# Weights loaded back to back in 8 KB runs, and the second product moved ahead: a schedule change in a fused retention and gated MLP kernel

## The chip, the cores and the metric

The kernel runs on one core of a Trainium2 chip. The metric is device time in microseconds (us), lower is better. All times are of single executions; a kernel's figure is the median of its executions, and each experiment ran in rounds beside the kernel before on the same chip. A run is called slow when it lies more than 1.5% above the fastest run of its kernel; verdicts use the fast runs alone.

## The reference, cut to what matters

```python
# q, k, v: (4 batches, 8 heads, 768 steps, 64)
for t in range(S):                                    # retention, a decay gamma per head
    state = gamma * state + outer(k[:, :, t], v[:, :, t])
    y[:, :, t] = scale * q[:, :, t] @ state
x = y as (3072 tokens, 512)
h = x @ w_in                                          # 512 x 2048
out = (h * cos(h)) @ w_out                            # 2048 x 512
```

The kernel works in *pairs*: pair p is one chunk of 128 steps for two batches, 12 pairs in all. Two pairs make a *group* of 512 tokens, 6 groups. For a pair TensorE does T (transposes of q and k), A (scores), after a mask on VectorE Y (output), and the state. For a group it then does F (x times w_in, 16 units of four 512-column matmuls, each followed by a cosine on ScalarE and a product on VectorE) and O (times w_out, 16 units of four matmuls). F and O units are nearly all of TensorE's work.

## The kernel before: the parts that matter

```python
w_in_sb = sb([128, KIN, DF], BF16, "w_in_sb")      # KIN = 4, DF = 2048
w_out_sb = sb([128, KOUT, DM], BF16, "w_out_sb")   # KOUT = 16, DM = 512

def load_w_in(r, n=512):                           # piece r: 512 columns
    nc.gpsimd.dma_start(
        out=w_in_sb[:, :, ts(r, n)],
        in_=moe_w_in[:, ts(r, n)].rearrange("(i p) f -> p i f", p=128))

def load_w_out(r):
    nc.gpsimd.dma_start(
        out=w_out_sb[:, ts(r, 4), :],
        in_=moe_w_out[ts(r, 512), :].rearrange("(f p) m -> p f m", p=128))
# ... cut ...
def unit_f(g, f):                                  # one F unit of a group
    bank = banks.take()
    for i in range(KIN):
        nc.tensor.matmul(bank, lhsT=w_in_sb[:, i, ts(f, 128)], rhs=xt[g % 2][:, i, :],
                         start=(i == 0), stop=(i == KIN - 1))
    act(bank, gt[g % 2][:, f, :])
    banks.give(bank)
# pair_f(p, r): the same for one pair, four units of 256 columns for piece r
# ... cut ...
load(nc.gpsimd, 1, ("k0", "q1", "k1", "v1"))       # DMA order: w_in between the pairs
load_w_in(0, 256)
load_w_in(1, 256)
load_w_in(1)
# ... loads of pairs 2 to 4, load_w_in(2), load_w_in(3), and only then:
for r in range(4):
    load_w_out(r)
# ... TensorE's order: pair 0, pair 1, F of group 0, pair 2, part of F, pair 3, F of group 1,
#     then O of group 0 beside pairs 4 and 5, then F of g and O of g-1 in turns
```

Of the kernel before, what the change touches and what calls it, by code (L numbers as in the profile page):

```python
# [30 lines left out]
def kernel(  # L31
# [9 lines left out]
    nc = tc.nc  # L41
# [8 lines left out]
    NP = B // 2 * NC  # L50
    NG = NP // 2
    PRE = 5
    PT = 5

    scale = 1.0 / math.sqrt(D)
    lg = [math.log(1.0 - 2.0 ** (-5.0 - h)) for h in range(H)]
# [10 lines left out]
    banks = Banks([psum.tile([128, 512], FP32, name=f"bank{i}") for i in range(7)])  # L67
# [37 lines left out]
    def load(eng, p, names):  # L105
        bp, c = divmod(p, NC)
        for n in names:
            t, src = SRC[n[0]]
            b = int(n[1])
            eng.dma_start(  # L110
                out=t[p % PRE][b],
                in_=src[2 * bp + b, :, ds(c * C, C)].rearrange("h t d -> t h d"))

    def load_w_in(r, n=512):
# [4 lines that stand above are left out]
    def load_w_out(r):  # L119
        nc.gpsimd.dma_start(  # L120
            out=w_out_sb[:, ts(r, 4), :],
            in_=moe_w_out[ts(r, 512), :].rearrange("(f p) m -> p f m", p=128))


    nc.gpsimd.iota(pos, pattern=[[C, NC]], base=1, channel_multiplier=1,
                   allow_small_or_imprecise_dtypes=True)
    load(nc.sync, 0, ("q0", "k0", "q1"))
    load(nc.sync, 1, ("q0", "v0"))
    load(nc.gpsimd, 0, ("k1", "v0", "v1"))
    make_identity(nc, ident)  # L130
    nc.vector.memset(zero, 0.0)
    nc.vector.memset(lnsc, math.log(scale))
# [17 lines left out]
    def conv_q(p, eng):  # L150
        for b in range(2):
            eng.tensor_tensor(out=qs[p % NB][:, b], in0=qf[p % PRE][b],  # L152
                              in1=bc(gq, p % NC), op=ALU.mult)

    def conv_v(p, eng):
        for b in range(2):
            eng.tensor_tensor(out=vs[p % NB][:, b], in0=vf[p % PRE][b],  # L157
                              in1=bc(gk, p % NC), op=ALU.mult)

    def conv_k(p, on_act):  # L160
        for b in range(2):
            if on_act:
                nc.scalar.copy(out=ks[p % NB][:, b], in_=kf[p % PRE][b])  # L163
            else:
                nc.vector.tensor_copy(out=ks[p % NB][:, b], in_=kf[p % PRE][b])

    def stage_t(p, split, fill=0):
        n = p % NB
        for b in range(2):
            if fill:  # L170
                warm(fill * b)
            bank = banks.take()
            tr = bank.bitcast(BF16).rearrange("p (w a t) -> p w a t", w=2, a=HP)
            for w, src in enumerate((qs[n], ks[n])):
                for a in range(HP):
                    nc.tensor.transpose(tr[:, w, a, :], src[:, b, 2 * a : 2 * a + 2, :], ident)
            if split is None or split and b == 1:
                nc.vector.tensor_copy(out=qkt[n][:, :, b], in_=tr)  # L178
            else:
                nc.scalar.copy(out=qkt[n][:, :, b], in_=tr)  # L180
            banks.give(bank)

    def stage_t_dma(p):
        n = p % NB
        for w, src in enumerate((qs[n], ks[n])):
            nc.sync.dma_start_transpose(
                out=qkt[n][:, w].rearrange("p b a t -> p (b a) t"),
                in_=src.rearrange("p b h d -> p (b h d)"))
# [75 lines left out]
    def unit_f(g, f):  # L264
        bank = banks.take()
        for i in range(KIN):
            nc.tensor.matmul(bank, lhsT=w_in_sb[:, i, ts(f, 128)], rhs=xt[g % 2][:, i, :],  # L267
                             start=(i == 0), stop=(i == KIN - 1))
        act(bank, gt[g % 2][:, f, :])
        banks.give(bank)  # L270

    def pair_f(p, r, parts=(0, 1)):

        g, hf = divmod(p, 2)
        for f in [4 * r + 2 * i for i in parts]:
            bank = banks.take()
            for e in range(2):
                for i in range(KIN):
                    nc.tensor.matmul(bank[:, ts(e, 256)], lhsT=w_in_sb[:, i, ts(f + e, 128)],  # L279
                                     rhs=xt[g % 2][:, i, ts(hf, 256)],  # L280
                                     start=(i == 0 and e == 0), stop=(i == KIN - 1),
                                     skip_group_check=True)
            act(bank, gt[g % 2][:, f : f + 2, ts(hf, 256)])
            banks.give(bank)
# [2 lines left out]

    def unit_o(g, j, part):
        if part == 0:
            o_bank[0] = banks.take()  # L290
        bank = o_bank[0]
        for f in range(4 * part, 4 * part + 4):
            nc.tensor.matmul(bank, lhsT=gt[g % 2][:, f, ts(j, 128)], rhs=w_out_sb[:, f, :],  # L293
                             start=(f == 0), stop=(f == KOUT - 1))
        if part == 3:
            o = ob[j % 4]
            bp, c = divmod(2 * g + j // 2, NC)
            dst = out[ds((2 * bp + j % 2) * S + c * C, C), :]
            if g == NG - 1 and j == 3:
                nc.vector.tensor_copy(out=o[:, ts(0, 256)], in_=bank[:, ts(0, 256)])  # L300
                nc.sync.dma_start(out=dst[:, ts(0, 256)], in_=o[:, ts(0, 256)])
                nc.scalar.copy(out=o[:, ts(1, 256)], in_=bank[:, ts(1, 256)])
                nc.scalar.dma_start(out=dst[:, ts(1, 256)], in_=o[:, ts(1, 256)])
            else:
                nc.scalar.copy(out=o, in_=bank)  # L305
                nc.sync.dma_start(out=dst, in_=o)
            banks.give(bank)
# [10 lines left out]
    def masks(p, items):  # L318
        for it in items:
            stage_m(p, it)  # L320

    load(nc.gpsimd, 1, ("k0", "q1", "k1", "v1"))
    load_w_in(0, 256)
    load_w_in(1, 256)
    load_w_in(1)
    load(nc.sync, 2, ("q0", "q1"))
    load(nc.sync, 4, ("q0", "q1", "v0"))
    conv_v(1, nc.gpsimd)
    load_w_in(2)
    load(nc.gpsimd, 2, ("k0", "k1"))  # L330
    load_w_in(3)
    load(nc.gpsimd, 2, ("v0", "v1"))
    load(nc.gpsimd, 3, ("k0", "q0", "k1", "q1"))
    conv_q(2, nc.gpsimd)
    conv_v(2, nc.gpsimd)
    load(nc.gpsimd, 3, ("v0", "v1"))
    for r in range(4):
        load_w_out(r)

    warm(10)  # L340
    conv_q(0, nc.vector)
# [7 lines left out]
    conv_q(1, nc.vector)  # L349
    warm(6)  # L350
    stage_y(0, nc.scalar.copy)
    conv_v(3, nc.gpsimd)
    load(nc.gpsimd, 4, ("k0", "k1", "v1"))
    warm(2)
    stage_t(1, None)
    m1 = stage_a(1)
# [2 lines left out]
    banks.give(spare)  # L359
    stage_y(1, nc.scalar.copy)  # L360
    pair_f(1, 0)
    for r in (1, 2):
        pair_f(0, r)
        pair_f(1, r)
    conv_k(2, True)
    pair_f(0, 3)
    stage_t(2, None)
    pair_f(1, 3, (0,))
    m2 = stage_a(2)
    masks(2, m2)  # L370
    pair_f(1, 3, (1,))
    stage_y(2, nc.scalar.copy)
    load(nc.sync, 5, ("q0", "q1", "v0"))
    conv_q(4, nc.gpsimd)
    load(nc.gpsimd, 5, ("k0", "k1", "v1"))
    pair_f(2, 0)
    conv_k(3, True)
    conv_q(3, nc.vector)
    pair_f(2, 1)
    stage_t(3, None)  # L380
    pair_f(2, 2, (0,))
    m3 = stage_a(3)
    masks(3, m3)
    pair_f(2, 2, (1,))
    pair_f(2, 3)
    stage_y(3, nc.scalar.copy)
    conv_v(4, nc.gpsimd)
    load(nc.sync, 6, ("q0", "q1", "v0"))
    load(nc.gpsimd, 6, ("k0", "k1", "v1"))
    for r in range(4):  # L390
        pair_f(3, r)
        if r == 2:
            conv_k(4, True)


    todo = []
    for g in range(1, NG + 1):
        for s in range(16):
            hf, r = divmod(s, 8)
            p = 2 * (g + 1) + hf  # L400
            if 1 < g < NG:
                unit_f(g, s)
            unit_o(g - 1, *divmod(s, 4))
            if p < NP:
                if r == 0 and p + 1 < NP:
                    conv_q(p + 1, nc.gpsimd)
                    conv_k(p + 1, True)
                    conv_v(p + 1, nc.gpsimd)
                elif r == 1 and p < PT:
                    stage_t(p, False)  # L410
                elif r == 2:
                    todo = stage_a(p)
                    stage_m(p, todo[0])
                    if PT <= p + 1 < NP:
                        stage_t_dma(p + 1)
                elif r == 3:
                    stage_m(p, todo[1])
                elif r == 6:
                    stage_y(p)
                    if p + 3 < NP:  # L420
                        load(nc.sync, p + 3, ("q0", "q1", "v0"))
                        load(nc.gpsimd, p + 3, ("k0", "k1", "v1"))


# [28 lines left out]
```

## Time and profile before

| | before |
|---|---|
| time, median of 3 (lowest to highest) | 219.75 us (219.67 to 219.83) |
| span of the profiled run, TensorE busy | 217.8 us, 94% |
| first F matmul | 15.8 us |
| first O matmul | 59.0 us |
| TensorE without a named wait from | about 63.7 us to the end |

These are three rows of the profile page's part 2 (the span in 40 slices of 5.4 us; a digit is the busy share in tenths; PEclk is the clock granted to TensorE, 9 meaning full or nearly; DMA is the load of the transfer engines):

```profile
PE   7687987879999999999999999999999999999993
...
PEclk9999999999999999999999999999999999999999
DMA  6999999999969999996951651051011001110212
```

TensorE is full from the tenth slice on; what is missing lies in the first 50 us, where the DMA engines are full too. The timeline of TensorE shows the waits (start, length, what, count, and in brackets the idle time ahead of it and what ended it). In these views PE is TensorE, PEld its weight loads, DVE VectorE, ACT ScalarE, POOL GpSimd and SPq Sync's queue. Of the tiles, qf, kf and vf are the loaded q, k and v, qs, ks and vs their converted forms, qkt the transposes, am the masked scores, xt the output Y as F reads it, gt the product h cos(h), and bank a buffer for matmul results:

```profile
15.80 1.05 PE L279 MATMUL bank<-xt,w_in_sb 128*128 128x256 bf16 x8
17.81 1.05 PE L279 MATMUL bank<-xt,w_in_sb 128*128 128x256 bf16 x8 [0.97 <-DMA w_in_sb<-in_moe_w_in_dram]
...
30.41 1.92 PE L279 MATMUL bank<-xt,w_in_sb 128*128 128x256 bf16 x16 [0.91 <-DMA w_in_sb<-in_moe_w_in_dram]
...
44.75 0.40 PE L176 MATMUL bank<-ident,qs 128*128 128x128 bf16 x4 [0.83 <-DVE qs L152]
...
58.99 1.89 PE L293 MATMUL bank<-w_out_sb,gt 128*128 128x512 bf16 x8
```

Each piece of w_in is waited for about 1 us at a time, and between 33 and 48 us it is conversions and copies on other engines that TensorE waits for. O, which needs little from the others, starts only at 59 us. The weight loads (LDWEIGHTS) and the 256-column matmuls that read w_in (duration in ns as min/median/max):

```profile
L279 PEld LDWEIGHTS <-w_in_sb x256: 95/98/99, 15.8 to 58.8; 128*128 128x128 bf16 x128
L279 PE MATMUL bank<-xt,w_in_sb x256: 269/273/283, 15.8 to 58.9; 128*128 128x256 bf16 x128
```

### The profile page before, as it was taken

To read this page: it belongs to the slowest core of one execution; us is meant where nothing else is said; L and a number is where in the kernel's file an instruction comes from. 1 tells how busy PE (TensorE), PEld (TensorE's weight loads), DVE (VectorE), ACT (ScalarE), POOL (GpSimd) and SP (SyncE) were. 2 spreads that over 40 slices of the span, in tenths; PEclk is the share of its full clock that TensorE was granted. 3 is DMA by queue.
4 is the path that set the end of the run, shared out by engine and by line. 5 is a ranking of instruction groups with operands and counts; after the bars stand their busy time and mean duration, and the time that the engine had idled before them with its cause. 6 is when DMAs were issued, how large, how long until landed. Compare 5 with 4: busy or idle time off the path is not lost.

```text
span 217.8 us, 4276 instructions
## 1 busy us (share of the span) xinstructions
PE 203.8 (94%) x1701; PEld 111.8 (51%) x1701; DVE 114.1 (52%) x185; ACT 116.1 (53%) x185; POOL 85.8 (39%) x98
## 2 busy tenths in 40 slices
PE   7687987879999999999999999999999999999993
PEld 2356875758855454544544544544544544444441
DVE  4595769596662417557448547647546244433000
ACT  5656784838874174464474564564534644454120
POOL 7969469982499991858160510000000000000000
PEclk9999999999999999999999999999999999999999
DMA  6999999999969999996951651051011001110212
GB/s 154 336 239 196 245 306 285 177 196 255 267 188 226 277 243 277 250 305 138 282 147 62 137 144 48 3 144 50 3 48 48 14 38 48 48 51 2 96 68 76
DMA packets 58676, 33.31 MB, mean 153 GB/s; under 512 B 48224, under 2 KB 53088, under 8 KB 58656
## 3 DMA queue, kind: packets, MB, share of 16 engines
q1 hardware_dynamic: 50480, 17.96, 34.8%
q0 software_dynamic: 8032, 14.95, 27.3%
q8 instruction: 13, 0.21, 0.4%
q10 hardware_dynamic: 144, 0.13, 0.2%
q14 instruction: 7, 0.06, 0.1%
HBM read 27.26 MB, written 6.29 MB: 154 GB/s over the span
## 4 chain that ended last, share of the span: by engine, by line
PE 75%; DMA 10%; DVE 5%; ACT 4%; POOL 2%; SPq 1%; issue 1%; DVEq 0%; ACTq 0%; POOLq 0%
PE bank L293 37%; PE bank L267 26%; DMA w_in_sb<-in_moe_w_in_dram 6%; PE bank L279 5%; DMA vf<-in_v_dram 4%; PE bank L205 2%; PE bank L228 2%; PE bank L233 2%; DVE gt L262 2%; ACT cosb L258 2%; SPq L110 1%; DVE am L214 1%; POOL vs L157 1%; DVE qkt L178 1%; DVE qs L152 1%
## 5 line engine op out<-in xcount | busy, mean ns | idle before, releaser
L262 DVE TENSOR_TENSOR gt<-bank,cosb 128x512 bf16<-128x512 f32 x96 | 65.9, 690 | 70.4 <-ACT cosb L258 70.4
L258 ACT ACTIVATE cosb<-bank,halfpi 128x512 bf16<-128x512 f32 x96 | 65.8, 687 | 63.2 <-PE bank L267 49.9
L293 PE MATMUL bank<-w_out_sb,gt 128*128 128x512 bf16 x384 | 94.3, 379 | 0.0
L267 PE MATMUL bank<-xt,w_in_sb 128*128 128x512 bf16 x256 | 65.8, 379 | 0.0
L293 PEld LDWEIGHTS <-gt 128*128 128x128 bf16 x384 | 37.2, 98 | 44.3
L267 PEld LDWEIGHTS <-w_in_sb 128*128 128x128 bf16 x256 | 24.1, 98 | 28.3
L279 PE MATMUL bank<-xt,w_in_sb 128*128 128x256 bf16 x256 | 29.6, 273 | 3.2 <-DMA w_in_sb<-in_moe_w_in_dram 1.9
L214 DVE TENSOR_TENSOR am<-bank,mask 128x512 bf16<-128x512 f32 x48 | 30.2, 682 | 4.5 <-issue 2.5
L157 POOL TENSOR_TENSOR vs<-vf,gk 128x512 bf16<-128x512 f32 x22 | 22.9, 1059 | 13.5 <-PE bank L279 7.4
L279 PEld LDWEIGHTS <-w_in_sb 128*128 128x128 bf16 x256 | 24.5, 98 | 6.9 <-DMA w_in_sb<-in_moe_w_in_dram 2.4
L152 POOL TENSOR_TENSOR qs<-qf,gq 128x512 bf16<-128x512 f32 x18 | 19.1, 1081 | 21.1 <-DMA qf<-in_q_dram 15.5
L110 POOL DMA_DIRECT2D kf<-in_k_dram x23 | 20.9, 910 | 3.2 <-DMA w_in_sb<-in_moe_w_in_dram 2.9
L305 ACT COPY ob<-bank 128x512 f32<-128x512 f32 x23 | 13.5, 586 | 16.3 <-PE bank L293 16.3
L237 ACT CAST xt<-bank 128x512 bf16<-128x512 f32 x24 | 13.0, 588 | 10.2 <-PE bank L233 10.2
L163 ACT CAST ks<-kf 128x512 bf16<-128x512 f32 x24 | 13.7, 615 | 4.2 <-DMA kf<-in_k_dram 4.2
L110 POOL DMA_DIRECT2D vf<-in_v_dram x15 | 13.3, 891 | 1.0 <-DMA w_out_sb<-in_moe_w_out_dram 1.0
L233 PE MATMUL bank<-am,vs 128*64 128x128 bf16 x192 | 12.1, 220 | 0.9 <-DVE am L214 0.9
L250 DVE CAST stb<-st_ps 64x512 bf16<-64x512 f32 x12 | 8.3, 689 | 6.5 <-PE st_ps L245 6.3
L228 PEld LDWEIGHTS <-stb 128*64 128x64 bf16 x160 | 8.7, 109 | 4.4 <-issue 4.4
L233 PEld LDWEIGHTS <-vs 128*64 128x64 bf16 x192 | 10.1, 110 | 1.5 <-issue 0.9
L228 PE MATMUL bank<-qkt,stb 128*64 128x128 bf16 x160 | 10.6, 222 | 0.0
L205 PE MATMUL bank<-qkt 64*128 64x128 bf16 x192 | 8.3, 218 | 2.1 <-DVE qkt L178 1.6
(38 smaller groups left out, 72.3 us busy)
## 6 DMA issues: line engine op xcount, KB each, us to landing
kf<-in_k_dram POOLq DMA_DIRECT2D x23, 256.0 KB, 5.9
out_dram<-ob SPq DMA_DIRECT2D x23, 256.0 KB, 2.1
qf<-in_q_dram SPq DMA_DIRECT2D x21, 256.0 KB, 7.2
vf<-in_v_dram POOLq DMA_DIRECT2D x15, 256.0 KB, 5.9
vf<-in_v_dram SPq DMA_DIRECT2D x9, 256.0 KB, 7.7
w_out_sb<-in_moe_w_out_dram POOLq DMA_DIRECT2D x4, 512.0 KB, 13.5
w_in_sb<-in_moe_w_in_dram POOLq DMA_DIRECT2D x3, 512.0 KB, 11.7
qf<-in_q_dram POOLq DMA_DIRECT2D x3, 256.0 KB, 8.7
```

What stands on the lines that cost most here:

```text
L110: eng.dma_start(out=t[p % PRE][b], in_=src[2 * bp + b, :, ds(c * C, C)].rearrange("h t d -> t h d"))
L152: eng.tensor_tensor(out=qs[p % NB][:, b], in0=qf[p % PRE][b], in1=bc(gq, p % NC), op=ALU.mult)
L157: eng.tensor_tensor(out=vs[p % NB][:, b], in0=vf[p % PRE][b], in1=bc(gk, p % NC), op=ALU.mult)
L163: nc.scalar.copy(out=ks[p % NB][:, b], in_=kf[p % PRE][b])
L214: nc.vector.tensor_tensor(out=am[p % 2][b][j], in0=ap[j], in1=mask.unsqueeze(1).to_broadcast([128, HP, 128]), op=ALU.mult)
L228: nc.tensor.matmul(yp[ts(j, 64), a, :], lhsT=stb[p % 2][:, b, a, ts(j, 64)], rhs=qt(n, b, a), start=True, stop=False, skip_group_check=True)
L233: nc.tensor.matmul(yp[ts(j, 64), a, :], lhsT=vs[n][:, b, 2 * a + j, :], rhs=am[p % 2][b][j][:, a, :], start=(c == 0), stop=True, skip_grou ...
L258: nc.scalar.activation(out=cb, in_=bank, func=AF.Sin, bias=halfpi)
L262: nc.vector.tensor_tensor(out=out, in0=bank, in1=cb, op=ALU.mult)
L267: nc.tensor.matmul(bank, lhsT=w_in_sb[:, i, ts(f, 128)], rhs=xt[g % 2][:, i, :], start=(i == 0), stop=(i == KIN - 1))
L279: nc.tensor.matmul(bank[:, ts(e, 256)], lhsT=w_in_sb[:, i, ts(f + e, 128)], rhs=xt[g % 2][:, i, ts(hf, 256)], start=(i == 0 and e == 0), s ...
L293: nc.tensor.matmul(bank, lhsT=gt[g % 2][:, f, ts(j, 128)], rhs=w_out_sb[:, f, :], start=(f == 0), stop=(f == KOUT - 1))
```

## The change

Its intent: give TensorE work that needs no other engine (O of group 0) while pairs 2 and 3 arrive. For that w_out must come early, so it is loaded right behind w_in, and in runs of 8 KB: partition p now holds rows 4p to 4p+3 of each block of 512. The F units must then use the matching columns of w_in, every fourth one, so its weight loads are strided by 8 bytes. O of group 1 is split, eight units ahead of group 2's turn and eight within it, and pair 4's transpose goes from TensorE to DMA.

```diff
-    PT = 5
+    PT = 4
@@ load_w_out
-            in_=moe_w_out[ts(r, 512), :].rearrange("(f p) m -> p f m", p=128))
+            in_=moe_w_out[ts(r, 512), :].rearrange("(p j) m -> p j m", j=4))
+
+    w_in_f = w_in_sb.rearrange("p i (r m j) -> p i r j m", r=4, j=4)
+
+    def w_in_t(i, f):
+        return w_in_f[:, i, f // 4, f % 4, :]
@@ loads of pairs 0 to 2 reordered (cut) @@ unit_f, pair_f
-            nc.tensor.matmul(bank, lhsT=w_in_sb[:, i, ts(f, 128)], rhs=xt[g % 2][:, i, :],
+            nc.tensor.matmul(bank, lhsT=w_in_t(i, f), rhs=xt[g % 2][:, i, :],
@@ order of the DMA queue
-    load_w_in(0, 256)
-    load_w_in(1, 256)
-    load_w_in(1)
-    (pairs 2 to 4 and w_in pieces 2 and 3 in turns, cut)
+    for r in range(4):
+        load_w_in(r)
     conv_v(1, nc.gpsimd)
     for r in range(4):
         load_w_out(r)
+    (loads of pairs 2, 3, 4, cut)
@@ order of TensorE's work
     pair_f(0, 0)
     banks.give(spare)
     stage_y(1, nc.scalar.copy)
     pair_f(1, 0)
-    for r in (1, 2):
-        pair_f(0, r)
-        pair_f(1, r)
+    for f in range(4, 16):
+        unit_f(0, f)
+    (conversions of pair 2)
+    for part in range(4):
+        for j in range(2):
+            unit_o(0, j, part)
+    unit_o(0, 2, 0)
+    unit_o(0, 2, 1)
     stage_t(2, None)
+    (rest of O of group 0 between A and Y of pair 2; then pair 3 in F of group 1, cut)
+    attend(4)
+    o_units(1, 0, 4)
+    later(4)
+    attend(5)
+    ahead(6)              # conversions of pair 6
+    stage_t_dma(6)        # its transposes, on Sync's DMA queue
+    o_units(1, 4, 8)
+    later(5)
+    (then F of g and O of g-1 in turns as before; 8 O units in group 2's turn)
```

More of the change, by code (lines that the diff above doesn't have):

```diff
@@ L121, in load_w_out @@
             out=w_out_sb[:, ts(r, 4), :],
-            in_=moe_w_out[ts(r, 512), :].rearrange("(f p) m -> p f m", p=128))
+            in_=moe_w_out[ts(r, 512), :].rearrange("(p j) m -> p j m", j=4))
+    w_in_f = w_in_sb.rearrange("p i (r m j) -> p i r j m", r=4, j=4)
+    def w_in_t(i, f):
+        return w_in_f[:, i, f // 4, f % 4, :]
+    load(nc.sync, 0, ("q0", "k0", "q1"))
+    load(nc.sync, 1, ("q0", "v0"))
+    load(nc.sync, 2, ("q0", "q1", "v0"))
+    load(nc.gpsimd, 0, ("k1",))
     nc.gpsimd.iota(pos, pattern=[[C, NC]], base=1, channel_multiplier=1,
                    allow_small_or_imprecise_dtypes=True)
-    load(nc.sync, 0, ("q0", "k0", "q1"))
-    load(nc.sync, 1, ("q0", "v0"))
-    load(nc.gpsimd, 0, ("k1", "v0", "v1"))
+    load(nc.gpsimd, 0, ("v0", "v1"))
     make_identity(nc, ident)
@@ L278, in pair_f @@
                 for i in range(KIN):
-                    nc.tensor.matmul(bank[:, ts(e, 256)], lhsT=w_in_sb[:, i, ts(f + e, 128)],
+                    nc.tensor.matmul(bank[:, ts(e, 256)], lhsT=w_in_t(i, f + e),
                                      rhs=xt[g % 2][:, i, ts(hf, 256)],
@@ L289, in unit_o @@
         if part == 0:
-            o_bank[0] = banks.take()
-        bank = o_bank[0]
+            o_bank[j] = banks.take()
+        bank = o_bank[j]
         for f in range(4 * part, 4 * part + 4):
@@ L322 @@
     load(nc.gpsimd, 1, ("k0", "q1", "k1", "v1"))
-    load_w_in(0, 256)
-    load_w_in(1, 256)
-    load_w_in(1)
-    load(nc.sync, 2, ("q0", "q1"))
-    load(nc.sync, 4, ("q0", "q1", "v0"))
-    conv_v(1, nc.gpsimd)
-    load_w_in(2)
-    load(nc.gpsimd, 2, ("k0", "k1"))
-    load_w_in(3)
-    load(nc.gpsimd, 2, ("v0", "v1"))
-    load(nc.gpsimd, 3, ("k0", "q0", "k1", "q1"))
-    conv_q(2, nc.gpsimd)
-    conv_v(2, nc.gpsimd)
-    load(nc.gpsimd, 3, ("v0", "v1"))
+    for r in range(4):
+        load_w_in(r)
+    conv_v(1, nc.gpsimd)
     for r in range(4):
         load_w_out(r)
+    load(nc.sync, 3, ("q0", "q1"))
+    load(nc.gpsimd, 2, ("k0", "k1", "v1"))
+    load(nc.gpsimd, 3, ("k0", "k1", "v0", "v1"))
+    load(nc.sync, 4, ("q0", "q1"))
+    load(nc.gpsimd, 4, ("k0", "k1", "v0", "v1"))
     warm(10)
@@ L351 @@
     stage_y(0, nc.scalar.copy)
-    conv_v(3, nc.gpsimd)
-    load(nc.gpsimd, 4, ("k0", "k1", "v1"))
     warm(2)
@@ L361 @@
     pair_f(1, 0)
-    for r in (1, 2):
-        pair_f(0, r)
-        pair_f(1, r)
+    for f in range(4, 16):
+        unit_f(0, f)
     conv_k(2, True)
-    pair_f(0, 3)
+    conv_q(2, nc.vector)
+    conv_v(2, nc.vector)
+    for part in range(4):
[3 more added lines that the diff above has]
+    unit_o(0, 2, 1)
     stage_t(2, None)
-    pair_f(1, 3, (0,))
+    unit_o(0, 2, 2)
     m2 = stage_a(2)
     masks(2, m2)
-    pair_f(1, 3, (1,))
+    conv_k(3, True)
@@ L372 @@
+    unit_o(0, 2, 3)
+    load(nc.sync, 5, ("q0", "q1", "v0"))
+    load(nc.gpsimd, 5, ("k0", "k1", "v1"))
+    for part in range(3):
+        unit_o(0, 3, part)
     stage_y(2, nc.scalar.copy)
-    load(nc.sync, 5, ("q0", "q1", "v0"))
+    unit_o(0, 3, 3)
+    conv_q(3, nc.vector)
+    conv_v(3, nc.gpsimd)
     conv_q(4, nc.gpsimd)
-    load(nc.gpsimd, 5, ("k0", "k1", "v1"))
+    conv_v(4, nc.gpsimd)
     pair_f(2, 0)
-    conv_k(3, True)
-    conv_q(3, nc.vector)
+    stage_t(3, None)
     pair_f(2, 1)
-    stage_t(3, None)
@@ L381 @@
-    pair_f(2, 2, (0,))
     m3 = stage_a(3)
     masks(3, m3)
-    pair_f(2, 2, (1,))
+    conv_k(4, True)
+    stage_t_dma(4)
+    load(nc.sync, 6, ("q0", "q1", "v0"))
+    load(nc.gpsimd, 6, ("k0", "k1", "v1"))
+    pair_f(2, 2)
     pair_f(2, 3)
     stage_y(3, nc.scalar.copy)
-    conv_v(4, nc.gpsimd)
-    load(nc.sync, 6, ("q0", "q1", "v0"))
-    load(nc.gpsimd, 6, ("k0", "k1", "v1"))
-    for r in range(4):
-        pair_f(3, r)
-        if r == 2:
-            conv_k(4, True)
-    todo = []
@@ L397, with attend, ahead, later @@
-    for g in range(1, NG + 1):
+    conv_q(5, nc.gpsimd)
+    conv_v(5, nc.gpsimd)
+    pair_f(3, 0)
+    conv_k(5, True)
+    stage_t_dma(5)
+    for r in range(1, 4):
+        pair_f(3, r)
+    def attend(p):
+        todo = stage_a(p)
+        masks(p, todo)
+    def ahead(p):
+        if p < NP:
+            conv_q(p, nc.gpsimd)
+            conv_k(p, True)
+            conv_v(p, nc.gpsimd)
+    def later(p):
+        stage_y(p)
+        if p + 3 < NP:
+            load(nc.sync, p + 3, ("q0", "q1", "v0"))
+            load(nc.gpsimd, p + 3, ("k0", "k1", "v1"))
@@ L398, with o_units @@
+    def o_units(g, a, b):
+        for u in range(a, b):
+            unit_o(g, *divmod(u, 4))
+    attend(4)
[6 more added lines that the diff above has]
+    later(5)
+    for g in range(2, NG + 1):
         for s in range(16):
@@ L400 @@
             p = 2 * (g + 1) + hf
-            if 1 < g < NG:
+            if g < NG:
                 unit_f(g, s)
-            unit_o(g - 1, *divmod(s, 4))
+            if g > 2:
+                unit_o(g - 1, *divmod(s, 4))
+            elif s % 2:
+                unit_o(1, *divmod(8 + s // 2, 4))
             if p < NP:
-                if r == 0 and p + 1 < NP:
-                    conv_q(p + 1, nc.gpsimd)
-                    conv_k(p + 1, True)
-                    conv_v(p + 1, nc.gpsimd)
-                elif r == 1 and p < PT:
-                    stage_t(p, False)
+                if r == 0:
+                    ahead(p + 1)
                 elif r == 2:
@@ L413 @@
                     stage_m(p, todo[0])
-                    if PT <= p + 1 < NP:
+                    if p + 1 < NP:
                         stage_t_dma(p + 1)
@@ L418 @@
                 elif r == 6:
-                    stage_y(p)
-                    if p + 3 < NP:
-                        load(nc.sync, p + 3, ("q0", "q1", "v0"))
-                        load(nc.gpsimd, p + 3, ("k0", "k1", "v1"))
+                    later(p)
 _INS = ['q', 'k', 'v', 'moe_w_in', 'moe_w_out']
```

## The prediction

> **What bounds it now.** TensorE. In the chain of waits, from 63.7 us to about 214 us nearly every piece is matmuls back to back (four of 512 columns every 0.86 us), then 3.8 us of copy and store. The granted clock is 1.00. The loss is in front: between the first F matmul (15.8 us) and 63.7 us I count 38.7 us of matmul work at back-to-back rates, so 9 us of stalls, 6.5 of them after 33 us. The timeline names them: w_in landing (1.0 us at 17.8, 0.9 at 30.4), xt copies (0.4 to 0.5 each), qkt copies and masks of pair 2 (34 to 38 us), qs of pair 3 (43 to 45 us). The DMA engines are saturated until about 60 us: w_in's last piece lands at 30.4, w_out's near 55 us.
>
> **What the change does.**
> 1. DMA order: w_in in four pieces, w_out right behind, then pairs 2 to 4. In the packet records a weight piece takes 512 packets, about 3.35 us beside a full second queue; a 256 KB load issued by GpSimd 64 packets, 0.82 us. Estimate: w_in lands at 17.0, 20.4, 23.7, 27.1 us. Packets of 1 KB source take 59 ns, of 2 KB 96 ns; on that line an 8 KB run takes 320 ns, a w_out piece 2.75 us, and the last lands near 38 us (40.5 if long runs gain nothing); k1 of pair 2 at 40 us.
> 2. PE order: group 0's F finishes near 32.7 us without a wait; ten O units (8.6 us) then cover the arrival of pair 2; T2 comes at about 41.5 us. Waits of T, A, masks and Y fall between O units, which need little of ScalarE and VectorE. One transpose on PE (0.9 us) becomes a DMA transpose.
> 3. Cost: Sync's q/v loads starve. Full queues move packet for packet (153 each per us); behind 8 KB packets Sync gets fewer. q of pair 3 comes only at about 50 us; conv_q(3) then holds VectorE and T3 about 1 us.
> 4. Strided LDWEIGHTS: w_in columns are now 8 bytes apart. [...] This trace has no strided weight load. Contiguous ones keep up with a 128-column matmul per 56 ns (transposes); at double cost they hide under 216 ns (512 columns) and nearly under 109 ns (256 columns, 160 such left). At four times they would cost about 17 us.
>
> **Sum.** F(2) starts near 78 us with 136 O/F units left; the old kernel at 77 us has 145: about 7 us gained. I take off 2 us for unforeseen waits around pairs 2 and 3, and 1 us for a slower w_out.
>
> Predicted 214.8 us; 8 in 10 between 212.0 and 218.5. Faster by over 2%: 0.55, within 2%: 0.38, slower: 0.07.
>
> **What would show it.** w_out's last landing under 41 us; PE without idle from 20.6 to about 40 us; T2 at 41 to 44 us; T3 waiting on qs; span about 213 us, the last 130 us unchanged in rate; w_in's LDWEIGHTS still about 98 ns and 256-column matmuls 0.109 us apart.
>
> **What would make it wrong.** Strided weight loads slower than 110 ns; w_out slower in long runs (PE waits at O's parts); Sync starvation delaying q of pair 3 beyond 55 us; GpSimd stuck behind q of pair 4, so that DMA transposes of pairs 4 and 5 pass 67 us.

The double and fourfold costs of a weight load in point 4 are suppositions of mine, set against the spacings of 56, 109 and 216 ns in the trace of the kernel before; nothing measured stood behind the factors.

## More of the kernel before

The framework adds the semaphore waits by itself: it looks at which tile regions an instruction reads and which earlier instructions write them. (A semaphore is what such a wait names; some of the waits of the built programs are listed under "The result".)

## The result

| | before | after |
|---|---|---|
| time, median (lowest to highest) | 219.79 us (219.67 to 220.72), 4 runs | 226.89 us (226.41 to 227.17), 4 runs |
| ratio of fast runs, 95% interval | | 1.0312 (1.0277 to 1.0346) |
| span of the profiled run, mean granted clock | 217.8 us, 1.000 | 225.5 us, 0.969 |

Here and below a ratio is the mean time of one kernel's fast runs over that of the other's in the same rounds, so it is not quite the ratio of the medians quoted. I had predicted 2% faster; it became 3% slower. The rows of the profile page of the changed kernel:

```profile
PE   7760099999999999899999999999999999999992
...
PEclk9997559999999999999999999999999999999999
```

Two slices of TensorE are empty, and the clock falls to half. Behind that it is fuller than before. The timeline of TensorE in the changed kernel:

```profile
17.43 0.30 PE L286 MATMUL bank<-xt,w_in_sb 128*128 128x256 bf16 x1 [0.41 <-DMA w_in_sb<-in_moe_w_in_dram]
28.26 3.37 PE L286 MATMUL bank<-xt,w_in_sb 128*128 128x256 bf16 x15 [10.53 <-DMA w_in_sb<-in_moe_w_in_dram]
...
34.15 1.91 PE L286 MATMUL bank<-xt,w_in_sb 128*128 128x256 bf16 x16 [0.25 <-ACT xt L244]
35.89 10.52 PE L274 MATMUL bank<-xt,w_in_sb 128*128 128x512 bf16 x48
46.25 8.80 PE L300 MATMUL bank<-w_out_sb,gt 128*128 128x512 bf16 x40
54.89 0.39 PE L183 MATMUL bank<-ident,qs 128*128 128x128 bf16 x4
```

The first piece of w_in is there at 17.4 us. *One* F matmul runs, and the second, of the same unit and the same piece, waits 10.5 us for "w_in". It goes on at 28.3 us, just after the *fourth* piece has landed (28.1 us). From then on the plan works: F, then ten O units, then pair 2's transposes without a gap. The table by stretches (busy time of each engine, then granted clock, DMA load, GB/s):

```profile
20.00:24.00 4.00, 0.00 (x0) 0.00 (x0) 0.00 (x0) 0.00 (x0) 0.90 (x1) 0.53 1.22 195
...
28.00:32.00 4.00, 3.74 (x25) 2.57 (x27) 0.69 (x1) 1.02 (x2) 1.76 (x2) 0.50 1.07 211
32.00:36.00 4.00, 3.75 (x61) 3.73 (x58) 0.75 (x2) 3.26 (x6) 0.88 (x1) 0.77 1.07 210
```

After the idle stretch the first work runs at clock 0.50: 15 matmuls of 256 columns took 3.37 us, where 16 take 1.91 us a little later. The clock records of this trace give half clock from 20.2 to 33.9 us: the clock fell 2.5 us after the last matmul had ended (17.7 us) and came back 5.6 us after the work had gone on (28.3 us). Whether the idle stretch is what lowers it is tested in e3.

The strided weight loads and their matmuls:

```profile
L286 PEld LDWEIGHTS <-w_in_sb x160: 111/113/152, 17.4 to 80.5; 128*128 128x128 bf16 x160
L286 PE MATMUL bank<-xt,w_in_sb x160: 269/273/421, 17.4 to 80.6; 128*128 128x256 bf16 x160
```

A strided weight load takes 113 ns and not 98, and the matmuls are not slower for it (273 ns in both kernels; 64 of them in a row take 7.15 us in both timelines). The maxima of 152 and 421 are those at half clock.

The cause can be read in the list of the program's own waits (this is the program, not the profile: position on TensorE, instruction, the load semaphores it waits for; semaphore 7 is w_in's first piece, 0, 1 and 2 the next three; the kernel before has five pieces, as its first 512 columns come in two):

```
before:  235 Ldweights w_in_sb [waits 7]        after:  235 Ldweights w_in_sb [waits 7]
         251 Ldweights w_in_sb [waits 0]                237 Ldweights w_in_sb [waits 2, 1, 0]
         395 Ldweights w_in_sb [waits 1]                (no more)
         ...
```

In a partition of w_in_sb element number is 2048 i + column. The second F weight load (i = 1) reads elements 2048, 2052, ..., 2556, all of piece 0. Piece 1 writes 512 to 1023, 2560 to 3071, and so on: not one element in common. But from its first to its last element piece 1 spans 512 to 7167, and the strided read lies inside that span. The first weight load (i = 0, elements 0 to 508) lies ahead of the spans of pieces 1, 2 and 3, and it waits for one piece only. So **theory A**: for a strided view the framework compares spans and adds waits that the data do not need. The rivals: **B**, the new order of the loads makes w_in really late; **C**, the strided weight loads are what costs time.

### The profile page after: what moved, and what is told of

The parts are those of the page before. It is cut to its first block, busy times and chain, and to the rows that moved or that the text cites. A ratio compares the mean times of both kernels' runs of the same rounds, so it can differ in the third digit from the quotient of the medians.

```text
span 225.5 us, 4141 instructions
## 1 busy us (share of the span) xinstructions
PE 204.4 (91%) x1637; PEld 114.7 (51%) x1637; DVE 116.3 (52%) x189; ACT 113.6 (50%) x183; POOL 78.1 (35%) x91
## 4 chain that ended last, share of the span: by engine, by line
PE 57%; DVE 0%; ACT 0%; issue 0%; DVEq 0%
PE bank L300 28%; PE bank L274 25%; PE bank L212 1%; PE bank L235 1%; PE bank L240 1%; PE st_ps L252 1%; DVE ob L307 0%; ACT ob L309 0%; DVEq L307 0%
## 5 line engine op out<-in xcount | busy, mean ns | idle before, releaser
L300 PE MATMUL bank<-w_out_sb,gt 128*128 128x512 bf16 x384 | 93.0, 379 | 0.0
L274 PE MATMUL bank<-xt,w_in_sb 128*128 128x512 bf16 x304 | 75.8, 380 | 0.7 <-ACT xt L244 0.7
L274 PEld LDWEIGHTS <-w_in_sb 128*128 128x128 bf16 x304 | 33.5, 114 | 30.7 <-issue 0.7
L286 PE MATMUL bank<-xt,w_in_sb 128*128 128x256 bf16 x160 | 20.2, 286 | 12.0 <-DMA w_in_sb<-in_moe_w_in_dram 10.9
L159 POOL TENSOR_TENSOR qs<-qf,gq 128x512 bf16<-128x512 f32 x16 | 16.5, 1042 | 36.1 <-DMA qf<-in_q_dram 25.0
L286 PEld LDWEIGHTS <-w_in_sb 128*128 128x128 bf16 x160 | 17.9, 116 | 13.5 <-issue 11.7
L164 POOL TENSOR_TENSOR vs<-vf,gk 128x512 bf16<-128x512 f32 x20 | 21.1, 1076 | 2.5 <-DMA vf<-in_v_dram 2.4
L240 PE MATMUL bank<-am,vs 128*64 128x128 bf16 x192 | 12.7, 227 | 1.0 <-DVE am L221 1.0
L240 PEld LDWEIGHTS <-vs 128*64 128x64 bf16 x192 | 10.7, 115 | 2.2 <-issue 1.7
L235 PEld LDWEIGHTS <-stb 128*64 128x64 bf16 x160 | 9.2, 115 | 4.0 <-issue 3.6
L322 PE MATMUL bank<-gt 128*128 128x512 bf16 x21 | 7.3, 500 | 1.3 <-DVE gt L138 1.3
```

The source lines that it names most:

```text
L159: eng.tensor_tensor(out=qs[p % NB][:, b], in0=qf[p % PRE][b], in1=bc(gq, p % NC), op=ALU.mult)
L164: eng.tensor_tensor(out=vs[p % NB][:, b], in0=vf[p % PRE][b], in1=bc(gk, p % NC), op=ALU.mult)
L235: nc.tensor.matmul(yp[ts(j, 64), a, :], lhsT=stb[p % 2][:, b, a, ts(j, 64)], rhs=qt(n, b, a), start=True, stop=False, skip_group_check=True)
L240: nc.tensor.matmul(yp[ts(j, 64), a, :], lhsT=vs[n][:, b, 2 * a + j, :], rhs=am[p % 2][b][j][:, a, :], start=(c == 0), stop=True, skip_grou ...
L274: nc.tensor.matmul(bank, lhsT=w_in_t(i, f), rhs=xt[g % 2][:, i, :], start=(i == 0), stop=(i == KIN - 1))
L286: nc.tensor.matmul(bank[:, ts(e, 256)], lhsT=w_in_t(i, f + e), rhs=xt[g % 2][:, i, ts(hf, 256)], start=(i == 0 and e == 0), stop=(i == KIN ...
```

## The experiments

All gave correct results. Runs e1 to e4 share one chip, e5 to e7 another, e8 to e10 the chip of e5 to e7, e11 and e12 a third chip.

### e1: the old layout alone

```diff
-            in_=moe_w_out[ts(r, 512), :].rearrange("(p j) m -> p j m", j=4))
+            in_=moe_w_out[ts(r, 512), :].rearrange("(f p) m -> p f m", p=128))
-        return w_in_f[:, i, f // 4, f % 4, :]
+        return w_in_sb[:, i, ts(f, 128)]
```

> The changed kernel with the old layout alone: w_in columns read contiguously, w_out in 2 KB runs; order of loads and of work as changed. Theory A (the strided view makes the second F weight load wait for all four pieces of w_in, a wait the data do not need): the 10.5 us wait at 17.7 us is gone, the clock stays 1.00, about 216 us (214 to 218.5). Rival B (the wait comes from the new order of the loads: w_in and w_out in one row fill the queue and w_in really is late): the wait stays, about 226 us.

Measured: 218.58 us median (217.41 to 220.94, the last a slow run), ratio to before 0.990 (0.982 to 0.997); the median is just above the range expected. The wait at 17.7 us is gone (16 F matmuls in a row from 17.48 us). B falls: with the same order of loads w_in is in time. The largest wait that remains is for w_out, in the timeline of TensorE of e1:

```profile
17.48 1.92 PE L286 MATMUL bank<-xt,w_in_sb 128*128 128x256 bf16 x16 [0.93 <-DMA w_in_sb<-in_moe_w_in_dram]
...
35.33 1.89 PE L300 MATMUL bank<-w_out_sb,gt 128*128 128x512 bf16 x8 [0.20 <-DMA w_out_sb<-in_moe_w_out_dram]
38.71 1.89 PE L300 MATMUL bank<-w_out_sb,gt 128*128 128x512 bf16 x8 [1.50 <-DMA w_out_sb<-in_moe_w_out_dram]
42.05 3.61 PE L300 MATMUL bank<-w_out_sb,gt 128*128 128x512 bf16 x16 [1.45 <-DMA w_out_sb<-in_moe_w_out_dram]
```

That is 3.2 us, because in 2 KB runs w_out lands later (its last piece at 42.0 us, against 38.8 in the changed kernel).

### e2: w_in in four tiles, one for each load

```diff
-    w_in_sb = sb([128, KIN, DF], BF16, "w_in_sb")
+    w_in_sb = [sb([128, KIN, 512], BF16, f"w_in_sb{r}") for r in range(4)]
-            out=w_in_sb[:, :, ts(r, n)],
+            out=w_in_sb[r],
-    w_in_f = w_in_sb.rearrange("p i (r m j) -> p i r j m", r=4, j=4)
+    w_in_f = [t.rearrange("p i (m j) -> p i j m", j=4) for t in w_in_sb]
-        return w_in_f[:, i, f // 4, f % 4, :]
+        return w_in_f[f // 4][:, i, f % 4, :]
```

> The changed kernel, w_in held in four tiles, one for each load; still read in strides, w_out still in 8 KB runs. Theory A: the second weight load of F waits for its own piece only, no idle at 17.7 us, clock 1.00, about 214.8 us (212 to 217.5). Rival B: unchanged, about 226 us. Rival C (strided weight loads themselves slow F): F units still cost more than in the kernel before, time well over 220 us.

Measured: 214.57 us in the profiled run, and 217.87, 219.47, 220.16 in the others. The wait is gone, with strided weight loads still in place. The profiled run's TensorE:

```profile
17.40 1.94 PE L286 MATMUL bank<-xt,w_in_sb 128*128 128x256 bf16 x16 [0.73 <-DMA w_in_sb<-in_moe_w_in_dram]
...
21.08 1.91 PE L286 MATMUL bank<-xt,w_in_sb 128*128 128x256 bf16 x16 [0.47 <-ACT xt L244]
22.82 10.52 PE L274 MATMUL bank<-xt,w_in_sb 128*128 128x512 bf16 x48
33.18 8.80 PE L300 MATMUL bank<-w_out_sb,gt 128*128 128x512 bf16 x40
41.82 0.39 PE L183 MATMUL bank<-ident,qs 128*128 128x128 bf16 x4
...
79.18 1.89 PE L274 MATMUL bank<-xt,w_in_sb 128*128 128x512 bf16 x8 [0.72 <-ACT xt L244]
```

In this run it is nearly the schedule that I had predicted for the change itself: F of group 0 done at 33.2 us (predicted 32.7), pair 2's transposes at 41.8 (41.5), F of group 2 at 79.2 (78). Its span of 212.9 us is 12.6 us shorter than the changed kernel's. The single wait is worth 10.5; e3 measures the rest. But this is the fastest of ten runs of this kernel (four here, six in e5), and their median is 219.7 us, outside the range expected: with the wait alone removed, a typical run is hardly faster than the kernel before (220.0 and 220.1 us). The clock alone does not explain the scatter: the run of 219.47 us had a mean granted clock of 1.000, that of 214.57 us 0.992. It is a new question (e5).

### e3: TensorE kept busy while it waits

```diff
+    warm(48)
     pair_f(0, 0)
     banks.give(spare)
```

> The changed kernel with 48 filler matmuls (10.4 us) ahead of the first F matmul, so that TensorE is busy while it waits. Expected: F goes on at about 28.3 us as in the changed kernel, but at a granted clock of 1.00; the 15 F matmuls, Y and state of pair 1 then take 2.8 us less (3.4, 1.7 and 0.6 us at half clock), so about 224 us. If the clock has no part in it: 226.9 us.

Measured: 224.82 us median (224.66 to 225.08), 2.1 us under the changed kernel's 226.89. They were run at other times. Against the kernel before the ratio is 1.020 (1.015 to 1.025), where the changed kernel had 1.031. The wait stays, the clock does not fall behind it. Its TensorE timeline, and then its table by stretches:

```profile
28.17 1.80 PE L286 MATMUL bank<-xt,w_in_sb 128*128 128x256 bf16 x15 [0.31 <-DMA w_in_sb<-in_moe_w_in_dram]
```

```profile
28.00:32.00 4.00, 3.36 (x66) 3.19 (x67) 1.38 (x2) 2.67 (x5) 1.77 (x2) 1.00 1.07 211
```

The same 15 matmuls that took 3.37 us take 1.80. So of the 12.6 us about 10.5 are the wait and 2.1 to 2.5 the half clock behind it: 2.1 by the medians, 2.5 by the spans of the profiled runs, 225.5 and 223.0 us (I had expected 2.8).

### e4: the kernel before with the layout alone

The layout of the change put into the kernel before (one w_in tile, strided reads, w_out in 8 KB runs; w_in's first piece loaded whole), with the old order of loads and work:

```diff
-    load_w_in(0, 256)
-    load_w_in(1, 256)
+    load_w_in(0)
     load_w_in(1)
-            in_=moe_w_out[ts(r, 512), :].rearrange("(f p) m -> p f m", p=128))
+            in_=moe_w_out[ts(r, 512), :].rearrange("(p j) m -> p j m", j=4))
-   lhsT=w_in_sb[:, i, ts(f, 128)]                   (both F functions)
+   lhsT=w_in_t(i, f)
```

> The kernel before with the layout alone: strided reads of w_in from one tile, w_out in 8 KB runs, first w_in piece whole; the old order of loads and work. Theory A: the second F weight load waits for the last piece of w_in, at about 30 us; 228 to 235 us. Rival B (order): no such wait, 219 to 221 us.

Measured: 238.21 us (237.87 to 239.06), ratio 1.080. TensorE of e4:

```profile
17.10 0.30 PE L284 MATMUL bank<-xt,w_in_sb 128*128 128x256 bf16 x1 [0.16 <-DMA w_in_sb<-in_moe_w_in_dram]
29.86 3.37 PE L284 MATMUL bank<-xt,w_in_sb 128*128 128x256 bf16 x15 [12.46 <-DMA w_in_sb<-in_moe_w_in_dram]
```

The same false wait in the old order, so the order has no part in it. It cost more than I expected, 18 us. Set beside e6, which differs in the four tiles alone: 14.5 us are lost by the F of pair 1 (35.1 against 20.6 us), and 4.2 us more by the F at 71.4 us (52.7 in e6). In that second stretch the waits for qs of pair 3 are 5.0 us and not 2.5, and the matmuls run at about half speed behind them (at 63.3 us 8 matmuls of 256 columns take 1.91 us, at 46.5 us 1.04; the run's mean granted clock is 0.950). Why qs comes later I have not followed.

### e6: the same in four tiles

e4's kernel with e2's edit (four w_in tiles).

> The old order with the new layout, w_in in four tiles (the layout alone, without the false wait). If the layout by itself is worth something only where O comes early, this stays at the time of before: 218.5 to 221 us (O starts at 59 us there, w_out had landed at 55). If strided weight loads cost TensorE time: over 222 us.

Measured: 220.36 us (219.28 to 221.19), ratio 1.002 (0.998 to 1.005). Without the false wait the layout alone neither costs nor gains anything that these runs show in the old order. C falls: the strided weight loads (113 ns each in the changed kernel's trace) cost no time that this run shows.

### e10: one tile, columns ordered by piece

```diff
-    w_in_sb = sb([128, KIN, DF], BF16, "w_in_sb")
+    w_in_sb = sb([128, 4, KIN, 512], BF16, "w_in_sb")
-            out=w_in_sb[:, :, ts(r, n)],
+            out=w_in_sb[:, r],
-    w_in_f = w_in_sb.rearrange("p i (r m j) -> p i r j m", r=4, j=4)
+    w_in_f = w_in_sb.rearrange("p r i (m j) -> p i r j m", j=4)
```

> The changed kernel with one w_in tile still, but its columns ordered by piece, so that each of the four loads writes one unbroken span of a partition; reads stay strided. If the false wait comes from spans that overlap (each load's writes lay scattered across the spans of the others), it is gone with one tile too: as the four-tile kernel, 214.5 to 220 us, F from 17.4 us. If one tile with strided reads is enough to cause it: 226 to 227 us.

Measured: 216.72 to 219.34 us in the fast runs and 221.68 in a slow one, ratio 0.988 (0.983 to 0.992). The list of waits shows one load semaphore at each first use of a piece, and F runs from 17.1 us without the long wait (the profiled run is the slow one; its lost time lies later, in a wait of 4.9 us for pair 2's copies):

```profile
17.11 1.94 PE L286 MATMUL bank<-xt,w_in_sb 128*128 128x256 bf16 x16 [0.73 <-DMA w_in_sb<-in_moe_w_in_dram]
```

One tile with strided reads is not enough to cause the wait; the spans must overlap. Nor are overlapping spans enough: in e1 the second weight load reads elements 2048 to 2175, inside piece 1's span too, but contiguously, and it does not wait. So it takes both. With this theory A holds down to its detail, though the comparison of spans is inferred from the lists of waits; I did not read the framework's code.

### e5: the four-tile kernel once more

No edit.

> The four-tile kernel once more, unchanged, because its four times lay between 214.6 and 220.2 us while the kernel before also wandered on that chip. If the spread belongs to that chip: within 0.5 us of 214.6 here. If it belongs to the kernel (its loads come just in time, so that small shifts of the transfers cost TensorE waits): again 214 to 220 us, in two or more groups, here too.

Measured: 216.37, 218.46, 219.96, 220.54, 221.35, 224.41 us. The scatter belongs to the kernel, though on this chip the kernel before had slow runs too (three of twelve at 223.7 to 225.7 us). The profiled run, a fast one at 218.46, shows two waits that were shorter in the 214.57 us run. First VectorE waits for v of pair 2 (7.5 us, against 4.1 there) and so is late with pair 2's copies, for which TensorE waits 1.2 us (no wait is listed there); then TensorE waits for pair 6's transpose (0.37 us there). With 0.5 us for w_out that is 3.5 of the 3.9 us between the two spans. The last view is the issue of that transpose on Sync's queue:

```profile
43.36 1.29 DVE L164 TENSOR_TENSOR vs<-vf,gk 128x512 bf16<-128x512 f32 x2 [7.52 <-DMA vf<-in_v_dram]
```

```profile
87.06 0.62 PE L212 MATMUL bank<-qkt 64*128 64x128 bf16 x16 [2.09 <-DMA qkt<-ks]
```

```profile
77.30 3.58 SPq L193 DMA_TRANSPOSE qkt<-qs  x1
80.98 1.49 SPq L193 DMA_TRANSPOSE qkt<-ks  x1
```

Pair 6's transposes stand in Sync's row behind an output store and the loads of pair 7, and are issued at 77 to 81 us for a use at about 85. In the run of 214.57 us they were issued no sooner:

```profile
77.92 2.18 SPq L193 DMA_TRANSPOSE qkt<-qs  x1
80.20 1.25 SPq L193 DMA_TRANSPOSE qkt<-ks  x1
```

But there the second landed at 83.1 us, and here at 87.0. So the late issue is common to both runs and leaves no slack; what differs is how long the transposes are under way. In the changed kernel these waits do not appear: the false wait gave all transfers 10 us of slack, which is probably also why its times are so even (not tested).

### e7: three Y stages one unit earlier

```diff
-    pair_f(0, 0)
+    pair_f(0, 0, (0,))
     banks.give(spare)
     stage_y(1, nc.scalar.copy)
+    pair_f(0, 0, (1,))
@@ Y of pair 3 ahead of pair_f(2, 3); Y of pair 5 ahead of the last O unit
```

> The four-tile kernel with three Y stages moved one unit earlier in TensorE's order, so that the copy of Y into xt (waits of 0.5, 0.8 and 0.7 us at 20.6, 60.0 and 78.5 us in the profile of the four-tile kernel) runs beside a unit that does not need it. Expected: those three waits go, 1.5 to 2 us less than the four-tile kernel of the same call, about 213 us at its best.

Measured: 214.41, 216.80, 217.28, 218.21, 218.56, 223.40 us, ratio 0.983 (0.978 to 0.989). The three waits are gone from its profile (a slow run, 218.56), but the scatter hides what they are worth, and the best time is no better than e2's. A miss as a measurement.

### e8 and e9: pair 6's conversions and transposes earlier

```diff
+    ahead(6)
+    stage_t_dma(6)
     attend(4)
     o_units(1, 0, 4)
     later(4)
     attend(5)
-    ahead(6)
-    stage_t_dma(6)
```

e9 is e2 with this edit, e8 is e7 with it.

> The four-tile kernel with only that one move (pair 6's conversions and DMA transposes earlier). Same question without the moved Y stages: no wait for pair 6's transpose at 83 to 87 us, times 214.5 to 217.5 us and closer together than the four-tile kernel's 214.6 to 224.4 us; otherwise unchanged.

> The kernel with the three Y stages moved, and in addition pair 6's conversions and DMA transposes put ahead of pair 4's attention in the order of the queues. In the profiled run before this one TensorE waited 2.9 us at 84 us for pair 6's transpose, which Sync issued only at 77 us, behind the output store and the loads of pair 7. If that late place in Sync's row makes the spread: transposes of pair 6 issued by 72 us, no wait for them, times within about 2 us of each other, 213 to 216 us. If the spread has another source: unchanged, 214 to 223 us.

Measured: e9 214.51, 214.59, 214.96, 215.04, 215.70 us and one slow run of 218.78, ratio 0.977 (0.973 to 0.980); e8 214.42 to 215.56 and one of 219.06, ratio 0.976 (0.973 to 0.980). Ten of twelve runs lie between 214.4 and 215.7 us, where of the 16 runs of e2, e5 and e7 two did. Sync's queue and TensorE in e9:

```profile
72.46 1.23 SPq L193 DMA_TRANSPOSE qkt<-qs  x1
73.78 1.26 SPq L193 DMA_TRANSPOSE qkt<-ks  x1
```

```profile
83.49 0.62 PE L212 MATMUL bank<-qkt 64*128 64x128 bf16 x16
```

The transposes go out 5 to 7 us sooner and land by 78.7 us, and pair 6's scores no longer wait. So the late place of pair 6's conversions and transposes made the larger part of the scatter (the edit moves both, and I did not separate them). e8 and e9 are equal: the moved Y stages are worth nothing measurable, although their three waits sum to 2.0 us in e9. Part of that turned into a longer wait for w_out (1.0 us in e8, 0.6 in e9); the rest I have not traced.

### e11: v0 of pair 2 on GpSimd's queue

```diff
-    load(nc.sync, 2, ("q0", "q1", "v0"))
+    load(nc.sync, 2, ("q0", "q1"))
-    load(nc.gpsimd, 2, ("k0", "k1", "v1"))
+    load(nc.gpsimd, 2, ("k0", "k1", "v0", "v1"))
```

This is e8 with the edit.

> The kernel with moved Y and early pair-6 transposes, and in addition v0 of pair 2 loaded by GpSimd behind w_out instead of by Sync. In the slow profiled run of the one-tile-by-piece kernel that load, starved on Sync's queue, landed only at 45.6 us and held VectorE 9.9 us and TensorE 4.9 us. If that is a second source of the spread: VectorE's wait for v0 stays under 4 us, all times within 1.5 us of each other, best about 214.4 us. If the slow runs (219 us) come from something else, such as the clock: one in six is still near 219 us.

Measured: 214.37 us median (213.92 to 215.43), no slow run, ratio 0.972 (0.968 to 0.976): the lowest median, but the interval overlaps those of e8 and e9. VectorE still waits for v, 5.5 us and not under 4:

```profile
40.99 1.52 DVE L164 TENSOR_TENSOR vs<-vf,gk 128x512 bf16<-128x512 f32 x2 [5.50 <-DMA vf<-in_v_dram]
```

In e8, without the edit, that wait is 5.5 us too, and VectorE is done with it at 42.1 us (here 42.5), so in a fast run the edit gains nothing there. That it has no run near 219 us proves little: e12, on the same chip and with v0 left on Sync, has none either.

### e12: the new order, early transposes, old layout

e1 with the edit of e9.

> The new order with the old layout (contiguous weight loads, w_out in 2 KB runs) and the early pair-6 transposes: with the early-transpose kernel of the run before it gives the worth of the layout alone in the new order. TensorE waited 3.2 us for w_out's pieces in the profile of the old-layout kernel: expected 217 to 218.5 us against 215.0. If the long runs are worth nothing: 215 us.

Measured: 217.04 us median (216.72 to 217.50), ratio 0.984 (0.979 to 0.989). Against e9's 0.977, from another chip, the layout is worth about 0.7%, or 1.6 us, in the new order. The two intervals overlap, so this rests on the waits more than on the times: TensorE waits 2.8 us for w_out here and 0.6 in e9. In e12's timeline of TensorE:

```profile
38.17 1.89 PE L300 MATMUL bank<-w_out_sb,gt 128*128 128x512 bf16 x8 [1.39 <-DMA w_out_sb<-in_moe_w_out_dram]
41.47 3.61 PE L300 MATMUL bank<-w_out_sb,gt 128*128 128x512 bf16 x16 [1.42 <-DMA w_out_sb<-in_moe_w_out_dram]
```

## Why the prediction was wrong

**The step that failed** is in the second point: "group 0's F finishes near 32.7 us without a wait". It finished at 46.3 us. I had worked out when the data land and taken for granted that TensorE waits for no more than its data, as it did before (one semaphore for each piece). With the strided view the program waits for all four pieces at the second weight load. The wait cost 10.5 us and the half clock after it 2.1 to 2.5 us; e2, which only takes the wait away, has in its best run the span of 212.9 us that I predicted as "about 213 us". My text looked at the strided view only for its cost on TensorE's read side; none of the things that it named as able to make it wrong was this one.

A term of the sum was too small as well, and the false wait hid it: the 2 us taken off "for unforeseen waits". With the false wait gone, the median of ten runs (e2, e5) was 219.7 us, 4.9 above the prediction; only after pair 6's conversions and transposes were moved (e9) was it 215.0.

Point by point:

- *What bounds it now*: held. What TensorE lost, it lost ahead of 64 us; the changed kernel's work is packed without gaps from 34 to 72 us.
- *Landing of w_in* (predicted 17.0 to 27.1 us): right within about 1 us. The first piece was there at 17.4 us, the last at 28.1.
- *w_out near 38 us, an 8 KB run 320 ns*: right. The packet records show 322 ns (96 ns for w_in's packets of 2 KB source), the last piece landed at 38.8 us, and O units waited for it between not at all (e2) and 1.0 us (e8). With 2 KB runs they waited 3.2 us (e1) and 2.8 us (e12).
- *Order worth about 7 us, less 2 for unforeseen waits and 1 for w_out*: right for the best run of the repaired kernel (214.57 us), not for its typical one. That e9 and e11 have medians of 215.0 and 214.4 us, beside 214.8 predicted, is partly luck: they hold further moves that the prediction did not have. The unforeseen waits were for pair 6's transpose and v of pair 2.
- *Sync's loads starve*: right. In w_in's stretch (17 to 26 us) both queues moved about 155 packets per us each, Sync's of 256 bytes beside w_in's of 96 ns; behind w_out's 8 KB runs, of 322 ns, both fell to about 53 (packet records, 30 to 34 us). That the two queues move equally many is shown for these stretches, and not why. q of pair 3 came at 51.4 us (predicted about 50), but no transpose waited for it. The victim was v0 of pair 2 (43.3 us in e5).
- *Strided weight loads*: predicted "still about 98 ns", measured 113 ns, above the 110 ns that I had named as a danger. It did no harm: that the matmuls keep their spacing was right, and e6 shows no loss of time.
- *The granted clock*: I did not consider it, having no idle stretch in my plan. It was 0.50 from 20.2 to 33.9 us.

What stays open: why e8 and e9 still have one run each near 219 us (their mean granted clock was 0.982 and 0.984, against 0.990 to 1.000 in the others, but neither was profiled; the kernel before has a slow run too, at 227 us), and how much v0 of pair 2 adds to the scatter: with w_out in 8 KB runs and v0 on Sync, it landed between 29.9 us (e7) and 45.6 us (e10) in the profiles.

## What to carry to other kernels

A strided view of a tile that several loads fill in interleaved spans can make the first reader wait for all of them (10.5 us in the changed kernel, 12.5 in e4): list the program's waits after any change of layout, and give each load its own tile or its own unbroken span. An idle stretch of TensorE of 10.5 us cost 2.1 to 2.5 us more than itself here, because the clock was at 0.50 behind it (until 33.9 us, 5.6 us after the work went on). And when a repaired schedule scatters, look for a transfer that is issued just in time behind unrelated ones in its queue; moving it earlier in program order made the gain reliable here in ten of twelve runs.
